# One more V block of the outer rounds kept in SBUF, with shared chain buffers

## Chip, cores and metric

The program runs on 1 core of a Trainium2 chip. The metric is the device time of one execution in microseconds (us), as a median of several. A single-core run counts as slow if it is over 1.5% above the fastest of the same kernel.

## The reference

Four layers, A B A B. Only A matters here: a recurrent attention over 64 segments of 32 rows, where each segment sees 8 memory rows that the segment before produced.

```python
def _A_ref(x, mem0, Wq, Wk, Wv, Wo, seg_len):   # Dm 640, 32 heads of 192, 8 memory rows
    mem = mem0
    for s in range(n_seg):                      # 64 segments, strictly in order
        xs = x[:, s * seg_len:(s + 1) * seg_len, :]
        h = jnp.concatenate([mem, xs], axis=1)  # 40 rows
        q, k, v = (jnp.einsum('btd,dhe->bhte', h, W) for W in (Wq, Wk, Wv))
        ...                                     # masked softmax attention
        o = jnp.einsum('bhte,hed->btd', o, Wo)
        mem = o[:, :M, :]                       # the next segment needs these 8 rows
        outs.append(o[:, M:, :])
```

## The kernel before

The four weight matrices do not fit SBUF together. The 32 heads go in 4 rounds of 8. A segment runs rounds 0 1 2 3, the next one 3 2 1 0, so that the outer rounds 0 and 3 alternate and the round at a segment's turn is used twice in a row. Each matrix of a round has 5 blocks of 128 x 1536 bf16 (393 KB). `SLOTS` says how many of them, in the outer rounds, share one slot between rounds 0 and 3 and are reloaded once per segment; all others are resident. Wo of the outer rounds shares one tile, `wo_end`.

```python
SLOTS = {"Q": 3, "K": 3, "V": 4}
...
def load_slot(m, r, b):
    if holds.get((m, b)) != r:
        holds[m, b] = r
        w = PW if m == "Q" else PW // 2
        for h in range(0, PW, w):
            nc.sync.dma_start(out=slot[m, b][:, h:h + w], in_=wview[m][:, b, PW * r + h:PW * r + h + w])
...
def project(hT, ps, m, n, s, steps):     # round n of the segment: 5 blocks, 4 column tiles each
    ...
    if n == 0 and b >= KC - ns:          # the outer block has been read: fetch the other outer round's
        load_slot(m, order[NR - 1], b)
```

One segment, cut to what the change touches:

```python
to_rows(q_or_k("Q", 0), "Q")             # project, copy to `raw` (two buffers), transpose into QT / KT
to_rows(q_or_k("K", 0), "K")
...                                       # V of round 0
for n in range(L):                        # L = 3
    raw = q_or_k("Q", n + 1)
    if n > 0:
        OT = attend(Ep, n - 1)            # PSUM -> OT, 80 columns of each of 6 chunks
        tails_after(n - 1)
        keep_tail(OT, otb, order[n - 1])  # GpSimd copies the 16 fetched columns; one store per segment
    S, E = weigh(False)                   # scores and exp
    to_rows(raw, "Q")
    next_kq(s, n)
    to_rows(q_or_k("K", n + 1), "K")
    sums(S, E); normalise(S, E)           # ones matmul, Ln, Exp, multiply
    if n > 0:
        wo_round(W, order[n - 1], OT, n == 1, False)
        if n == 1:
            load_wo(order[L])             # wo_end: six pieces, last in the DMA queue
    ...                                   # V of the next round
...
wo_round(W, order[L], OT, False, True)    # reads wo_end piece by piece
keep_busy(idle, 3)                        # three idle matmuls
hT = hN                                   # second hT buffer, its 24 own rows transposed earlier
nc.vector.transpose(out=wt, in_=W ...)    # the 8 memory rows
nc.vector.tensor_copy(out=hT[:, :, 0:8], in_=wt[:, :, 0:8])
```

The softmax here doesn't subtract the row's maximum and nothing guards it: scores larger than these inputs give would overflow.

## Time and profile before

| | before |
|---|---|
| time, median of 3 | 4140.39 us (4123.13 to 4148.61) |
| two recurrent stages, first to last hT cast (62 of 64 segments) | 1424 us each |
| traffic | 986 MB, 238 GB/s over the span |
| slot reloads of V | 1072 DMAs of 192 KB |

The page's row for the wo_end matmuls, with busy time and mean ns, then the idle time just before them and what ended it, is

```profile
L767 PE MATMUL ps_w<-wo_end,OT 128*32 128x160 bf16 x12288 | 316.2, 236 | 168.7 <-DMA wo_end<-wo_rows 123.3
```

The idle column, and not the DMA's share of the chain, is the gap that the prediction counts.

### The profile page before, as it was taken

Reading aid. Unit: us, or ns where it says so; the run is one execution under the profiler, and the core shown is the slowest. Engines: PE = TensorE matmul, PEld = TensorE weight load, DVE = VectorE, ACT = ScalarE, POOL = GpSimd, SP = SyncE. Lnnn points to the kernel's source line nnn. Section 1 sums busy time; section 2 is a strip of 40 time slices with the busy share of each in tenths; the row PEclk is TensorE's granted clock in tenths of the full one; section 3 lists DMA queues with packets and bytes.
Section 4 is the critical chain, followed back from the end, with each engine's and each line's share of the span. In section 5 each row is a group of like instructions: output and inputs, shape, how many; then the busy total and the mean of one; then the engine's idle time right before and its main releaser. Section 6 shows DMA issues by size and latency. Waiting matters only on the chain.

```text
span 4141.3 us, 167399 instructions
## 1 busy us (share of the span) xinstructions
PE 3626.9 (88%) x70296; PEld 2253.0 (54%) x70312; DVE 2139.8 (52%) x5054; ACT 1882.1 (45%) x4461; POOL 1595.1 (39%) x4511
## 2 busy tenths in 40 slices
PE   4889999999999999869879799999999999998598
PEld 3655555555555555535357455555555555555353
DVE  4235555555555555445732455555555555553574
ACT  1235555555555555415312355455545455554252
POOL 1024544454455455330000345445545555542400
PEclk9999999999999999979989999999999999999798
DMA  8878888888888888830077888888878888887200
GB/s 260 250 230 286 273 283 277 280 281 277 283 278 284 275 286 293 285 89 1 31 251 213 268 278 282 265 287 284 286 266 284 275 293 282 282 277 242 86 1 26
DMA packets 642175, 986.34 MB, mean 238 GB/s; under 512 B 152202, under 2 KB 468106, under 8 KB 641418
## 3 DMA queue, kind: packets, MB, share of 16 engines
q1 hardware_dynamic: 497546, 861.82, 61.2%
q0 software_dynamic: 55936, 60.51, 5.3%
q10 hardware_dynamic: 87936, 53.30, 4.7%
q8 instruction: 551, 9.03, 0.9%
q14 instruction: 206, 1.69, 0.1%
HBM read 907.09 MB, written 72.09 MB: 236 GB/s over the span
## 4 chain that ended last, share of the span: by engine, by line
PE 63%; DMA 25%; DVE 4%; issue 3%; ACT 3%; POOL 1%; SPq 1%; ACTq 1%; POOLq 0%; DVEq 0%
PE ps_qk L702 21%; DMA wo_end<-wo_rows 15%; PE ps_v L702 8%; PE ps_w L767 6%; PE ps_pre L613 4%; PE ps_s L742 3%; PE ps_o L750 3%; DMA wslotV<-in_A_Wv_dram 3%; PE ps_qk L342 2%; PE ps_s L794 2%; PE pp L923 2%; PE ps_s L737 2%; PE ps_pre L628 2%; DMA kqb<-wo_mid 2%; PE ps_wo L455 2%
## 5 line engine op out<-in xcount | busy, mean ns | idle before, releaser
L702 PEld LDWEIGHTS <-hT 128*32 128x32 bf16 x30720 | 752.7, 98 | 528.2 <-issue 86.6
L702 PE MATMUL ps_qk<-w_res,hT 128*32 128x384 bf16 x14336 | 783.5, 332 | 1.3 <-issue 0.9
L712 ACT ACTIVATE raw<-ps_qk 128x384 bf16<-128x384 f32 x1024 | 501.7, 490 | 570.4 <-PE ps_qk L702 568.4
L767 PEld LDWEIGHTS <-OT 128*32 128x32 bf16 x24576 | 432.5, 97 | 321.1 <-issue 242.7
L685 POOL DMA_DIRECT2D Vp<-vb x512 | 261.5, 511 | 765.4 <-PE ps_o L750 286.7
L767 PE MATMUL ps_w<-wo_end,OT 128*32 128x160 bf16 x12288 | 316.2, 236 | 168.7 <-DMA wo_end<-wo_rows 123.3
L673 POOL DMA_DIRECT2D kqb<-kqb x512 | 290.6, 568 | 335.4 <-DMA kqb<-wo_mid 162.7
L717 DVE STREAM_TRANSPOSE KT<-raw 128x384 bf16<-128x384 bf16 x512 | 296.1, 578 | 177.2 <-ACT raw L712 173.4
L720 DVE STREAM_TRANSPOSE QT<-raw 128x256 bf16<-128x256 bf16 x512 | 228.0, 445 | 298.7 <-ACT raw L712 287.7
L731 DVE CAST Vp<-ps_v 64x384 bf16<-64x384 f32 x512 | 286.1, 559 | 139.0 <-ACT Vp L729 126.7
L702 PE MATMUL ps_v<-w_res,hT 128*32 128x384 bf16 x6144 | 345.0, 329 | 1.7 <-issue 1.5
L678 POOL COPY QT<-kqb 128x64 bf16<-128x64 bf16 x512 | 123.2, 241 | 564.9 <-PE ps_s L742 562.5
L756 DVE CAST OT<-ps_o 128x240 bf16<-128x240 f32 x512 | 208.8, 408 | 244.2 <-PE ps_o L750 228.0
L801 DVE TENSOR_TENSOR E<-E,ps_s 80x320 bf16<-80x320 bf16 x512 | 247.6, 484 | 145.3 <-ACT ps_s L800 145.1
L729 ACT ACTIVATE Vp<-ps_v 64x384 bf16<-64x384 f32 x512 | 246.1, 481 | 162.4 <-PE ps_v L702 162.3
L750 PEld LDWEIGHTS <-Vp 80*128 80x128 bf16 x4096 | 181.9, 100 | 188.7 <-issue 127.6
L750 PE MATMUL ps_o<-E,Vp 80*128 80x80 bf16 x4096 | 252.7, 203 | 32.2 <-DVE Vp L731 23.4
L767 PE MATMUL ps_w<-wo_mid,OT 128*32 128x160 bf16 x12288 | 266.1, 234 | 4.3 <-issue 3.8
L755 ACT ACTIVATE OT<-ps_o 128x240 bf16<-128x240 f32 x512 | 188.2, 368 | 166.7 <-PE ps_o L750 162.0
L780 ACT ACTIVATE E<-ps_s 80x320 bf16<-80x320 f32 x512 | 221.3, 432 | 87.0 <-PE ps_s L742 72.0
L702 PE MATMUL ps_v<-wslotV,hT 128*32 128x384 bf16 x4096 | 245.4, 334 | 2.5 <-DMA wslotV<-in_A_Wv_dram 2.2
L774 PE MATMUL ps_idle<-wo_mid,ident 128*128 128x384 bf16 x1024 | 242.5, 340 | 1.5 <-issue 1.5
(146 smaller groups left out, 5824.6 us busy)
## 6 DMA issues: line engine op xcount, KB each, us to landing
wo_end<-wo_rows SPq DMA_DIRECT2D x780, 320.0 KB
wslotV<-in_A_Wv_dram SPq DMA_DIRECT2D x1072, 192.0 KB
wslotK<-in_A_Wk_dram SPq DMA_DIRECT2D x804, 192.0 KB
wslotQ<-in_A_Wq_dram SPq DMA_DIRECT2D x402, 384.0 KB
kqb<-wo_mid ACTq DMA_DIRECT2D x16, 1536.0 KB
kqb<-kqb POOLq DMA_DIRECT2D x512, 48.0 KB, 5.0
vb<-wo_end ACTq DMA_DIRECT2D x128, 112.0 KB
Vp<-vb POOLq DMA_DIRECT2D x512, 28.0 KB, 4.8
```

The lines of the kernel that those rows point to most:

```text
L673: nc.gpsimd.dma_start(out=kqb[:], in_=self.kqb_d[s, :, r, :])
L685: nc.gpsimd.dma_start(out=Vs[n % 2][64:80, :], in_=self.vb_d[s, r].rearrange("g t f -> (g t) f"))
L702: nc.tensor.matmul(o[32 * g:32 * g + 32, 0:384], lhsT=hT[:, b, :], rhs=rhs, start=(i == 0), stop=(i == KC - 1), tile_position=(0, 32 * g), ...
L712: nc.scalar.activation(out=raw[:], in_=ps[:, 0:384], func=ACT.Copy)
L717: nc.vector.transpose(out=KT[:, :, 0:64], in_=raw[:, :].rearrange("p (c j) -> p c j", j=64))
L720: nc.vector.transpose(out=QT[:, :, 0:4:3, 0:64], in_=rv[:, :, 0:3:2, :])
L729: nc.scalar.activation(out=o, in_=i, func=ACT.Copy)
L731: nc.vector.tensor_copy(out=o, in_=i)
L750: nc.tensor.matmul(O[x][:, 80 * i:80 * i + 80], lhsT=Vs[n % 2][0:80, 448 * x + k:448 * x + k + 128], rhs=E[0:80, 160 * x + 80 * e:160 * x ...
L767: nc.tensor.matmul(W[32 * g:32 * g + 32, 0:160], lhsT=OT[:, c, q:q + 32], rhs=w[:, 640 * i + 160 * g:640 * i + 160 * g + 160], start=(firs ...
L774: nc.tensor.matmul(ps[:, 0:384], lhsT=self.ident[:, :], rhs=wo_mid[:, 0:384], start=True, stop=True, skip_group_check=True)
L801: nc.vector.tensor_tensor(out=E[0:80, 0:320], in0=E[0:80, 0:320], in1=rc, op=ALU.mult)
```

## The change

The aim is to reload three V blocks per segment, not four. One more resident V block for each of rounds 0 and 3, less the slot they shared, needs 3072 B more per partition. It is found by using one buffer where two were, and by putting rows in unused partitions of the V tiles.

```diff
-SLOTS = {"Q": 3, "K": 3, "V": 4}
+SLOTS = {"Q": 3, "K": 3, "V": 3}
...
-        ones = const.tile([P, 80], BF16, name="ones_blk")
+        ones = const.tile([P, 1], BF16, name="ones_blk")          # read with a stride of 0
...
-            Hx = sp.tile([P, 2, 160], BF16, name="Hx")
+            xr, orow = [t[96:P, 0:640] for t in Vs]                # rows 96 to 127 of the V tiles
...
-                hT = sp.tile([P, KC, 32], BF16, name="hT", tag="hT", bufs=2)
-                nc.vector.transpose(out=hT[:, :, :], in_=Hx[:, s % 2, :].rearrange(...))
+            def hx_transpose(hT, gs):                              # one hT buffer, four transposes
+                for g in gs:
+                    nc.vector.transpose(out=hT[32 * g:32 * g + 32, :, :], in_=xr[:, 160 * g:160 * g + 160]...)
...
+            def keep_rows(W):                                      # four ACT copies of 32 partitions, one store
+                    nc.scalar.activation(out=orow[:, 160 * g:160 * g + 160], in_=W[32 * g:32 * g + 32, 0:160], ...)
...
-                raw = sp.tile([P, 384], BF16, name="raw", tag="raw", bufs=2)
+                raw = sp.tile([P, 384], BF16, name="raw", tag=tag)   # one buffer; K of round 0 takes OT's
...
-                OT = sp.tile([P, 6, 80], BF16, name="OT", tag="OT")
+                OT = sp.tile([P, 6, 64], BF16, name="OT", tag="OT")
...
-            def keep_tail(OT, otb, r):
-                nc.gpsimd.tensor_copy(out=otb[:, r, :, :], in_=OT[:, :, 64:80])
+            def keep_tail(o, late=False):                          # fetched columns straight from PSUM
+                ... nc.scalar.activation / nc.vector.tensor_copy(out=otb[:, 0:3, :], in_=o[0][:, :, 64:80])
+                nc.vector.tensor_copy(out=otb[:, 3:6, :], in_=o[1][:, :, 64:80])
+            def store_tail(otb, s, r):                             # four stores of 24 KB per segment
...
-                normalise(S, E)                                     # last round: VectorE multiplies, then copies its V rows
-                v_rows(pv, L)
+                v_rows(pv, L, "x")                                  # VectorE's V rows first
+                normalise(S, E)
+                v_rows(pv, L, "a")                                  # ScalarE's V rows
...
-    (next segment's hT transposed before the last V projection)
+                hx_transpose(hT, range(1))                          # before the last attend
+                ...
+                hx_transpose(hT, range(1, 4))                       # after it
```

More of the change, by code (lines that the diff above doesn't have):

```diff
@@ L645, in A_chain @@
             Vs = [sp.tile([P, 896], BF16, name=f"Vp{i}") for i in range(2)]
-            Hx = sp.tile([P, 2, 160], BF16, name="Hx")
-            for i, t in enumerate((KT, QT, *Vs, Hx)):
+            xr, orow = [t[96:P, 0:640] for t in Vs]
+            for i, t in enumerate((KT, QT, *Vs)):
                 (nc.vector if i % 2 else nc.gpsimd).memset(t[:], 0.0)
             xv = xn_dram.rearrange("(s t) d -> t s d", t=32)
-            av = at_dram.rearrange("(s t) d -> t s d", t=32)
             def rounds(s):
@@ L658, in load_rows, with new_hT, store_rows @@
             def load_rows(s):
-                for g in range(4):
-                    nc.gpsimd.dma_start(out=Hx[32 * g + 8:32 * g + 32, :, :], in_=xv[0:24, s:s + 2, 160 * g:160 * g + 160])
-            def hx_transpose(s):
-                hT = sp.tile([P, KC, 32], BF16, name="hT", tag="hT", bufs=2)
-                nc.vector.transpose(out=hT[:, :, :], in_=Hx[:, s % 2, :].rearrange("p (j b) -> p b j", b=KC))
-                return hT
-            def store_rows(s, ob):
-                for g in range(4):
-                    nc.gpsimd.dma_start(out=av[0:24, s:s + 2, 160 * g:160 * g + 160], in_=ob[32 * g + 8:32 * g + 32, :, :])
+                nc.gpsimd.dma_start(out=xr[8:32, :], in_=xn_dram[32 * s:32 * s + 24, :])
+            def hx_transpose(hT, gs):
+                for g in gs:
+                    nc.vector.transpose(out=hT[32 * g:32 * g + 32, :, :],
+                                        in_=xr[:, 160 * g:160 * g + 160].rearrange("p (j b) -> p b j", b=KC))
+            def new_hT():
+                return sp.tile([P, KC, 32], BF16, name="hT", tag="hT")
+            def keep_rows(W):
+                for g in range(4):
+                    nc.scalar.activation(out=orow[:, 160 * g:160 * g + 160], in_=W[32 * g:32 * g + 32, 0:160], func=ACT.Copy)
+            def store_rows(s):
+                nc.gpsimd.dma_start(out=at_dram[32 * s:32 * s + 24, :], in_=orow[8:32, :])
             def load_kqb(s, r):
@@ L708, in values, with to_raw @@
                 project(hT, pv, "V", n, s, steps)
-            def to_raw(ps):
-                raw = sp.tile([P, 384], BF16, name="raw", tag="raw", bufs=2)
+            def to_raw(ps, tag):
+                raw = sp.tile([P, 384], BF16, name="raw", tag=tag)
                 nc.scalar.activation(out=raw[:], in_=ps[:, 0:384], func=ACT.Copy)
@@ L722, in to_rows, with v_rows @@
                     nc.vector.transpose(out=QT[64:P, :, 2, 0:64], in_=rv[64:P, :, 1, :])
-            def v_rows(pv, n):
+            def v_rows(pv, n, which="ax"):
                 for x in range(2):
+                    if "ax"[x] not in which:
+                        continue
                     o = self.two_heads(Vs[n % 2][0:64, 448 * x:448 * x + 448])
@@ L752, in attend @@
                                          stop=(k == 192), skip_group_check=True)
-                OT = sp.tile([P, 6, 80], BF16, name="OT", tag="OT")
-                OTf = OT[:, :, :].rearrange("p c q -> p (c q)")
-                nc.scalar.activation(out=OTf[:, 0:240], in_=O[0][:, 0:240], func=ACT.Copy)
-                nc.vector.tensor_copy(out=OTf[:, 240:480], in_=O[1][:, 0:240])
-                return OT
-            def keep_tail(OT, otb, r):
-                nc.gpsimd.tensor_copy(out=otb[:, r, :, :], in_=OT[:, :, 64:80])
+                OT = sp.tile([P, 6, 64], BF16, name="OT", tag="OT")
+                o = [x[:, 0:240].rearrange("p (i q) -> p i q", q=80) for x in O]
+                nc.scalar.activation(out=OT[:, 0:3, :], in_=o[0][:, :, 0:64], func=ACT.Copy)
+                nc.vector.tensor_copy(out=OT[:, 3:6, :], in_=o[1][:, :, 0:64])
+                return OT, o
+            def keep_tail(o, late=False):
+                otb = sp.tile([P, 6, 16], BF16, name="otb", tag="otb", bufs=2)
+                if late:
+                    nc.vector.tensor_copy(out=otb[:, 0:3, :], in_=o[0][:, :, 64:80])
+                else:
+                    nc.scalar.activation(out=otb[:, 0:3, :], in_=o[0][:, :, 64:80], func=ACT.Copy)
+                nc.vector.tensor_copy(out=otb[:, 3:6, :], in_=o[1][:, :, 64:80])
+                return otb
+            def store_tail(otb, s, r):
+                nc.gpsimd.dma_start(out=self.otb_d[s, :, 96 * r:96 * r + 96], in_=otb[:, :, :].rearrange("p c t -> p (c t)"))
             def wo_round(W, r, OT, first, last):
@@ L778, in weigh @@
                 S = scores()
-                E = sp.tile([P, 384], BF16, name="E3", tag="raw", bufs=2) if last else sp.tile([P, 320], BF16, name="E", tag="E")
+                E = sp.tile([P, 384], BF16, name="E3", tag="raw") if last else sp.tile([P, 320], BF16, name="E", tag="E")
                 nc.scalar.activation(out=E[0:80, 0:320], in_=S[0:80, 0:320], func=ACT.Exp, scale=scale)
@@ L793, in sums @@
             def sums(S, E):
-                nc.tensor.matmul(S[0:80, 0:320], lhsT=self.ones_blk[0:80, :], rhs=E[0:80, 0:320], start=True, stop=True,
+                nc.tensor.matmul(S[0:80, 0:320], lhsT=ap3(self.ones_blk[0:80, :], [list(self.ones_blk[0:80, :].ap[0]), [0, 80]]), rhs=E[0:80, 0:320], start=True, stop=True,
                                  skip_group_check=True)
@@ L801, in normalise @@
                 nc.vector.tensor_tensor(out=E[0:80, 0:320], in0=E[0:80, 0:320], in1=rc, op=ALU.mult)
-            for g in range(4):
-                nc.gpsimd.dma_start(out=Hx[32 * g:32 * g + 8, 0, :], in_=self.A_mem0[:, 160 * g:160 * g + 160])
+            nc.gpsimd.dma_start(out=xr[0:8, :], in_=self.A_mem0[:, :])
             load_rows(0)
@@ L812, in A_chain @@
             kqs.append(load_kqb(0, rounds(0)[2]))
-            hT = hx_transpose(0)
-            otb = ob = None
+            hT = new_hT()
+            hx_transpose(hT, range(4))
+            load_rows(1)
             for s in range(NSEG):
-                if s % 2 == 0:
-                    ob_old, ob = ob, sp.tile([P, 2, 160], BF16, name="ob", tag="ob")
                 W = pop.tile([P, 512], F32, name="ps_w", tag="w")
@@ L824, in q_or_k @@
                     project(hT, ps, m, n, s, range(KC))
-                    return to_raw(ps)
+                    return to_raw(ps, "OT" if m == "K" and n == 0 else "raw")
                 def v_banks():
@@ L838, in A_chain @@
                 if s > 0:
-                    nc.gpsimd.dma_start(out=self.otb_d[s - 1], in_=otb[:, :, :, :].rearrange("p r c t -> p (r c t)"))
-                    if s % 2 == 0:
-                        store_rows(s - 2, ob_old)
+                    store_rows(s - 1)
                 pv = v_banks()
@@ L844, in A_chain @@
                 v_rows(pv, 0)
-                otb = sp.tile([P, NR, 6, 16], BF16, name="otb", tag="otb")
                 Ep = None
@@ L849, in A_chain @@
                     if n > 0:
-                        OT = attend(Ep, n - 1)
+                        OT, o = attend(Ep, n - 1)
                         tails_after(n - 1)
-                        keep_tail(OT, otb, order[n - 1])
                     S, E = weigh(False)
                     to_rows(raw, "Q")
+                    if n > 0:
+                        otb = keep_tail(o)
                     next_kq(s, n)
+                    if n > 0:
+                        store_tail(otb, s, order[n - 1])
                     to_rows(q_or_k("K", n + 1), "K")
@@ L870, in A_chain @@
                 S, E = weigh(True)
-                if s + 1 < NSEG:
-                    hN = hx_transpose(s + 1)
                 pv = v_banks()
                 project(hT, pv, "V", L, s, range(3))
-                OT = attend(Ep, L - 1)
+                OT, o = attend(Ep, L - 1)
                 tails_after(L - 1)
-                keep_tail(OT, otb, order[L - 1])
+                otb = keep_tail(o, True)
                 next_kq(s, L)
+                store_tail(otb, s, order[L - 1])
                 sums(S, E)
                 project(hT, pv, "V", L, s, range(3, KC))
+                v_rows(pv, L, "x")
                 normalise(S, E)
-                v_rows(pv, L)
+                v_rows(pv, L, "a")
+                if s + 1 < NSEG:
+                    hT = new_hT()
+                    hx_transpose(hT, range(1))
                 wo_round(W, order[L - 1], OT, False, False)
@@ L885, in A_chain @@
                 keep_busy(idle, 2)
-                OT = attend(E, L)
+                OT, o = attend(E, L)
                 tails_after(L)
-                keep_tail(OT, otb, order[L])
-                if s % 2 == 0 and s + 2 < NSEG:
-                    load_rows(s + 2)
+                if s + 1 < NSEG:
+                    hx_transpose(hT, range(1, 4))
+                    if s + 2 < NSEG:
+                        load_rows(s + 2)
                 keep_busy(idle, 3)
@@ L894, in A_chain @@
                 if s + 1 < NSEG:
-                    hT = hN
-                    wt = sp.tile([P, KC, 32], F32, name="wt", tag="raw", bufs=2)
+                    wt = sp.tile([P, KC, 32], F32, name="wt", tag="raw")
                     nc.vector.transpose(out=wt[:, :, :], in_=W[:, 0:160].rearrange("p (j b) -> p b j", b=KC))
                     nc.vector.tensor_copy(out=hT[:, :, 0:8], in_=wt[:, :, 0:8])
-                nc.scalar.activation(out=ob[:, s % 2, :], in_=W[:, 0:160], func=ACT.Copy)
-            nc.gpsimd.dma_start(out=self.otb_d[NSEG - 1], in_=otb[:, :, :, :].rearrange("p r c t -> p (r c t)"))
-            store_rows(NSEG - 2, ob)
+                store_tail(keep_tail(o), s, order[L])
+                keep_rows(W)
+            store_rows(NSEG - 1)
     def A_post(self, at_dram, li, wo_mid, wo_end, big):
```

## The prediction

> **What bounds the kernel now.** I read the page's slices and chain first, then the stages, then one segment instruction by instruction, then the waits of that segment's end.
>
> Parts 2 and 4 of the page:
>
> ```profile
> PE   4889999999999999869879799999999999998598
> DMA  8878888888888888830077888888878888887200
> GB/s 260 250 230 286 273 283 277 280 281 277 283 278 284 275 286 293 285 89 1 31 251 213 268 278 282 265 287 284 286 266 284 275 293 282 282 277 242 86 1 26
> ...
> PE 63%; DMA 25%; DVE 4%; issue 3%; ACT 3%; POOL 1%; SPq 1%; ACTq 1%; POOLq 0%; DVEq 0%
> ```
>
> TensorE and the DMA engines are both nearly full through most of the span, and the chain alternates between them. The two recurrent stages (64 segments each) fill 285 to 1709 us and 2337 to 3761 us; their table of busy times is
>
> ```profile
> 285.00:1709.00 1424.00, 1319.56 (x31249) 818.86 (x31247) 785.42 (x1922) 738.41 (x1798) 712.87 (x2042) 0.98 0.84 281
> 2337.00:3761.00 1424.00, 1317.51 (x31249) 817.74 (x31247) 785.68 (x1922) 738.25 (x1798) 712.83 (x2042) 0.98 0.84 281
> ```
>
> The columns are span, then busy time of PE, PEld, DVE, ACT and POOL, then granted clock, DMA share and GB/s. So 2848 of 4141 us lie here, DMA 84% busy, PE 93%. The chain of waits in one segment names the loop (start us, us, what):
>
> ```profile
> 1017.66 0.57 PE ps_v L702 x9
> 1018.23 6.65 DMA wo_end<-wo_rows
> 1024.89 0.04 issue
> 1024.93 0.35 PE ps_w L767 x8
> 1025.30 0.36 DVE wt L897
> 1025.68 0.20 DVE hT L898
> ```
>
> The next segment cannot begin before its memory rows (hT), which come from the whole ps_w sum, which needs the last piece of wo_end, which stands last in the DMA queue behind this segment's Q, K and V blocks. The 6.65 us is no stall: TensorE worked through most of it. Its true stall is the idle before the wo_end matmuls, in the timeline of PE:
>
> ```profile
> 1021.64 0.78 PE L767 MATMUL ps_w<-wo_end,OT 128*32 128x160 bf16 x24
> 1023.09 0.32 PE L767 MATMUL ps_w<-wo_end,OT 128*32 128x160 bf16 x8 [0.66 <-DMA wo_end<-wo_rows]
> 1024.20 0.32 PE L767 MATMUL ps_w<-wo_end,OT 128*32 128x160 bf16 x8 [0.80 <-DMA wo_end<-wo_rows]
> 1024.93 0.32 PE L767 MATMUL ps_w<-wo_end,OT 128*32 128x160 bf16 x8 [0.40 <-DMA wo_end<-wo_rows]
> ```
>
> Here it is 1.86 us. Summed by group over the first stage, then over the second:
>
> ```profile
> L767 PE MATMUL ps_w<-wo_end,OT 128*32 128x160 bf16 x5952 | 152.6, 237 | 78.5 <-DMA wo_end<-wo_rows 54.0 <-issue 22.0 <-ACT OT L755 1.4
> ...
> L767 PE MATMUL ps_w<-wo_end,OT 128*32 128x160 bf16 x5952 | 152.1, 235 | 78.0 <-DMA wo_end<-wo_rows 58.2 <-issue 19.2
> ```
>
> That is 156 us. **It is the most that fewer bytes can give directly.** DMA sets the period, but TensorE is only some 1.3 us per segment behind it.
>
> From the trace's records I cut both stages at the hT cast into 124 segments: mean period 22.97 us; first weight packet 1.69 us after the cast; stream from there to the last wo_end packet 19.67 us (6.31 MB, 321 GB/s, engines 95% busy, standard deviation 0.79 us); 1.61 us from there to the next cast. The DMA engines rest only in the turn between segments.
>
> **What the Trainium skill says.** "DMA: Bandwidth & Descriptors", section Issuing engines are not separate DMA queues: transfers from SP, ACT and GpSimd share 16 engines and interleave. The trace agrees: the segments' stream is 95% busy over all queues together, so a byte less anywhere in it shortens it. The same page, Specifications, sets 512 B as the smallest line-rate transfer. The trace does not show a penalty at 320 B: the 15 KB row transfers have packets of four such rows at a median 55 ns (23 B/ns), the old 768 B tail rows run at 4608 B in 206 ns (22 B/ns). The new 192 B rows are untested here. "TensorE: Matmul & The Clock Gate", What's actually happening: an activity window of 3413 ns halves the clock after idling. The clock records agree in form: they hold 0.5 stretches of 3.4 us, and the stages' mean is 0.98. "PSUM — Partial Sum Buffer", PSUM bank collisions: two engines' reads of one bank are kept apart by waits. It shows: ACT's ob copy waited for DVE's wt, both reading ps_w, for 426 us in the wait list.
>
> **The change part by part.**
> 1. *One V block (round 0 and round 3) stays resident; V reloads 3 blocks a segment, not 4.* Removed: two DMAs of 192 KB, that is 256 packets of 1536 B. At 71 ns a packet (mean in the records) over 16 engines: 1.14 us busy, 1.20 us of stream at 95%. By rate: 0.393 MB at 321 GB/s is 1.22 us. All of it precedes wo_end in the queue. Over two layers of 64 segments that is 50 MB of 986.
> 2. *Tail rows leave by four DMAs of 24 KB instead of one of 96 KB.* Same bytes, but the old one went at the segment's turn (POOL issued it at 1024.74 us), where the engines were resting; three of the new ones fall into the stream: 74 KB, 0.23 us. The row loads and stores become 24 rows of 1280 B in place of 320 B pieces, and some of the loads that ran beside the last wo_end pieces (packets up to 0.3 us long there) get simpler: I credit 0.1 us. **Stream shorter by 1.1 us net.**
> 3. *raw has one buffer instead of two (K of the first round borrows OT's).* ACT's copy of K must now wait for DVE's three Q transposes. In the segment shown, ACT began it at 1015.96 and DVE ended at 1016.06: with the hand-over 0.15 us later in each of three rounds. Scores follow KT's end (1017.07) with PE at 1017.21, and the attend at 1009.52 follows E's end at 1009.40, so about 0.1 us of TensorE delay in two places: 0.15 us.
> 4. *hT has one buffer, filled by four 32-partition transposes instead of one of 128.* One takes 352 ns now and its free size does not change, so 1.4 us, placed after the last V projection. Three follow the OT copy (ends near 1021.7), so DVE is free near 1022.7; without a DMA stall ps_w would end near 1022.6. 0.1 us.
> 5. *Tail copies go from POOL (275 ns each, gone) to ACT and DVE, from PSUM; OT is copied 192 wide, not 240.* Both have idle there (ACT 52%, DVE 55% busy in the stages); the OT copies, on the path, get some 0.04 us shorter.
> 6. *The row copy becomes four ACT copies of 32 partitions*, about 1.2 us in place of 0.3, after DVE's wt. ACT's next work came 1.29 us after the hT cast began (1002.43 to 1003.72): it just fits. No cost.
> 7. The ones matrix as a stride-0 column: one weight load of 114 ns a round, loaded ahead; no cost.
>
> TensorE's own loop thus grows by about 0.2 us (3, 4, less 5). The matmul count does not change.
>
> **Sum.** For each of the 124 segments, gain = stall less the larger of 0.2 and (stall less 1.1). The 156 us of stalls are uneven (quartiles 0.76, 1.29, 1.76 us), so the mean gain is 0.78 us rather than 0.9: 98 us over 126 turns. Clock: 51 segments with a halved stretch average 23.38 us, the other 73 22.69 us; 51 x 0.69 is 35 us, and with the stalls mostly gone I expect under half of it back, 15 us. The preparation stage reloads one block less per layer: 2 us. Together 115 us: **4025 us**, 2.8% less.
>
> **Rivals.**
> - *TensorE's chain becomes the bound early.* If the single raw buffer, the hT transposes and the row copies cost 0.5 us a segment, the same sum gives 75 us, and without clock gain 4063 us, within 2%. For it: slacks of 0.1 us in four places. Against it: each is a small shift beside idle time.
> - *The 192 B rows are slow.* If each took twice its bytes' time the stream shortens by 0.8 us; with 0.2 us on TensorE 76 us remain; with 2 us of preparation and half the clock gain (7 us) that is about 4055 us. Against it: 320 B rows show no loss.
> - *Proportional DMA gain.* If DMA alone set the period, 1.2 us x 128 and the 15 us of clock would give 3970 us. Against it: the stall is below 1.1 us in over a third of the segments, so TensorE catches up.
> - *Hidden anyway:* the chain's 25% DMA overstates; but 156 us of real idle exist, so "same" needs the new costs above.
>
> **Range and chances.** Low end: 1.22 us net, no TensorE cost, all clock loss back: 118 + 35 + 2 us, 3985 us, and some luck: 3975. High end: 0.95 us, 0.5 us cost, no clock gain: 70 us, 4070 us, and run-to-run spread (4123 to 4149 before): 4080. The 2% line is 4058 us, which leaves 33 us of margin against a doubt of some 40: faster 0.77, same 0.22, slower 0.01.
>
> **What would show it.** Right: wslotV moves a quarter less; the stream falls to about 18.6 us; idle before the wo_end matmuls falls from 156 to 50 to 75 us; period near 22.1 us; more segments wait for nothing; clock at or above 0.98. Wrong step 2: the new tail stores' packets exceed 100 ns each. Wrong steps 3 to 6: PE idle before ps_s, ps_o or the first ps_qk, or wt waiting for DVE's own transposes. The prediction fails above all if a new wait on raw, OT or hT puts over 0.5 us in every segment.

## The result

| | before | after |
|---|---|---|
| median | 4133.17 us, 4 runs | 4009.80 us, 4 runs (3987.02 to 4029.03) |
| ratio, 95% interval | 1 | 0.9696 (0.9633 to 0.9760) |
| stages, first to last hT cast | 1424.2, 1424.2 us | 1360.7, 1356.7 us |
| V reloads of 192 KB | 1072 | 804 |
| traffic | 986 MB | 935 MB |

Ratios are the mean time of one kernel's fast runs over the mean of the other's in the same rounds, so they are not quite the ratio of the medians. The changed kernel is faster by 3.0%, 123 us by the medians; its result is correct. Of the 127 us between the two profiled spans (4141.3 and 4014.4 us), 131 us came from the stages, and 4 us were lost outside them.

Slices and chain of the page after:

```profile
PE   4889999999999999869879799999999999998598
DMA  7777888788887888730076788788887887885200
GB/s 266 242 240 255 272 272 280 270 281 284 271 281 265 287 284 270 253 91 1 35 256 206 256 273 279 264 288 281 276 282 267 282 283 262 280 275 194 87 1 27
...
PE 62%; DMA 18%; DVE 6%; ACT 6%; issue 4%; POOL 2%; SPq 1%; ACTq 1%; POOLq 0%; DVEq 0%
```

The rate hardly changes (277 and 276 GB/s in the stages, 281 before); there is less to move. In the chain DMA falls from 25 to 18%, and DVE and ACT together rise from 7 to 12%: in some segments the chain now runs through the softmax and the copies. The row of the wo_end matmuls on the page after, and the stages' table:

```profile
L782 PE MATMUL ps_w<-wo_end,OT 128*32 128x160 bf16 x12288 | 291.2, 236 | 64.6 <-DMA wo_end<-wo_rows 32.4
...
285.00:1640.00 1355.00, 1292.20 (x31124) 813.19 (x31120) 887.89 (x2409) 811.77 (x2162) 674.82 (x1851) 0.99 0.82 277
2264.00:3619.00 1355.00, 1290.32 (x31136) 812.85 (x31136) 888.02 (x2410) 811.45 (x2162) 675.78 (x1853) 0.99 0.82 276
```

The idle time before them fell from 168.7 to 64.6 us over the whole span. Their busy time fell too, from 316.2 to 291.2 us, with the same count and the same mean of 236 ns: the matmuls overlap more when fewer waits break their row. So the idle column leaves out a part of what a wait costs. DVE has about 100 us more to do in each stage, ACT 73 us, POOL 38 us less; TensorE has the same matmuls. The waits of the segment's end, in the timeline of PE after:

```profile
1029.81 0.45 PE L756 MATMUL ps_o<-E,Vp 80*128 80x80 bf16 x8 [0.33 <-DMA Vp<-vb]
1030.09 0.66 PE L789 MATMUL ps_idle<-wo_mid,ident 128*128 128x384 bf16 x3
1030.67 0.97 PE L782 MATMUL ps_w<-wo_end,OT 128*32 128x160 bf16 x40
1032.50 0.32 PE L782 MATMUL ps_w<-wo_end,OT 128*32 128x160 bf16 x8 [0.85 <-DMA wo_end<-wo_rows]
```

Here five of the six pieces of wo_end are there in time and only the last is awaited, 0.85 us; in the segment of the prediction three of six were late.

To see where a segment's time goes, the trace's records were cut at the hT cast, as in the prediction: 124 segments, means in us. "First" runs from the cast to the first weight packet, "stream" from there to the last wo_end packet, "turn" from there to the next cast; the three add up to the period. "Stall" is TensorE's idle time before the wo_end matmuls, and the last column counts the segments that hold over 0.1 us of a halved-clock stretch, in which the records grant TensorE half its clock. The experiments are in the same table.

| kernel | period | first | stream | turn | stall | halved |
|---|---|---|---|---|---|---|
| before | 22.97 | 1.69 | 19.67 | 1.61 | 1.26 | 51 |
| after | 21.91 | 1.63 | 18.51 | 1.77 | 0.45 | 18 |
| e1, all but the V block | 22.86 | 1.66 | 19.61 | 1.59 | 1.08 | 40 |
| e2, the V block's bytes alone | 21.76 | 1.63 | 18.39 | 1.74 | 0.47 | 9 |
| e3, before, one block more | 24.32 | 1.79 | 21.05 | 1.48 | 1.76 | 95 |
| e4, after, one block less | 21.44 | 1.60 | 17.34 | 2.50 | 0.06 | 2 |
| e9, after again | 21.80 | 1.59 | 18.39 | 1.82 | 0.44 | 5 |
| e11, after with two repairs | 21.74 | 1.62 | 18.39 | 1.74 | 0.45 | 11 |
| e12, before with fillers | 23.14 | 1.63 | 19.80 | 1.71 | 0.74 | 24 |

The stream lost 1.16 us, the turn gained 0.16 us, and that is nearly the whole change of the period, 1.06 us. In the segments with all 504 matmul records (88 before, 105 after), TensorE reaches the last round's wo_end matmuls only 0.05 us sooner than before, and from their start to their end it takes 0.96 us less.

### The profile page after: what moved, and what is told of

Same layout as the page of the kernel before. It is cut to its first block, busy times and chain, and to the rows that moved or that the text cites. A ratio compares the mean times of both kernels' runs of the same rounds, so it can differ in the third digit from the quotient of the medians.

```text
span 4014.4 us, 168003 instructions
## 1 busy us (share of the span) xinstructions
PE 3588.7 (89%) x70296; PEld 2252.9 (56%) x70312; DVE 2357.3 (59%) x6078; ACT 2040.1 (51%) x5229; POOL 1516.4 (38%) x4119
## 4 chain that ended last, share of the span: by engine, by line
PE 62%; DMA 18%; DVE 6%; ACT 6%; issue 4%; POOL 2%; SPq 1%; ACTq 1%; POOLq 0%; DVEq 0%
PE ps_qk L706 18%; DMA wo_end<-wo_rows 10%; PE ps_w L782 8%; PE ps_v L706 6%; PE ps_pre L613 4%; PE ps_o L756 4%; PE ps_s L748 3%; PE ps_s L809 2%; PE ps_qk L342 2%; PE pp L939 2%; PE ps_s L743 2%; PE ps_pre L628 2%; DMA kqb<-wo_mid 2%; PE ps_wo L455 2%; PE ps_idle L789 2%
## 5 line engine op out<-in xcount | busy, mean ns | idle before, releaser
L706 PEld LDWEIGHTS <-hT 128*32 128x32 bf16 x30720 | 741.9, 97 | 493.2 <-DVE hT L914 53.4
L706 PE MATMUL ps_qk<-w_res,hT 128*32 128x384 bf16 x14336 | 769.1, 328 | 1.1 <-ACT otb L770 0.6
L706 PE MATMUL ps_v<-w_res,hT 128*32 128x384 bf16 x7168 | 385.0, 328 | 0.0
L775 POOL DMA_DIRECT2D otb<-otb x512 | 283.8, 554 | 181.7 <-DVE otb L771 137.5
L782 PE MATMUL ps_w<-wo_end,OT 128*32 128x160 bf16 x12288 | 291.2, 236 | 64.6 <-DMA wo_end<-wo_rows 32.4
L762 DVE CAST OT<-ps_o 128x192 bf16<-128x192 f32 x512 | 183.2, 358 | 236.8 <-PE ps_o L756 218.6
L756 PE MATMUL ps_o<-E,Vp 80*128 80x80 bf16 x4096 | 235.3, 202 | 38.7 <-DMA Vp<-vb 9.0
L748 PE MATMUL ps_s<-QT,KT 128*80 128x80 bf16 (+1 forms) x3072 | 234.3, 213 | 19.2 <-DVE KT L721 12.1
```

The costliest lines, as they stand in the source:

```text
L706: nc.tensor.matmul(o[32 * g:32 * g + 32, 0:384], lhsT=hT[:, b, :], rhs=rhs, start=(i == 0), stop=(i == KC - 1), tile_position=(0, 32 * g), ...
L748: nc.tensor.matmul(S[0:80, c0:c0 + 80 * (q1 - q0)], lhsT=KT[:, 3 * x + i, :], rhs=QT[:, x, q0:q1, :], start=False, stop=(x == 1 and i == 2 ...
L756: nc.tensor.matmul(O[x][:, 80 * i:80 * i + 80], lhsT=Vs[n % 2][0:80, 448 * x + k:448 * x + k + 128], rhs=E[0:80, 160 * x + 80 * e:160 * x ...
L775: nc.gpsimd.dma_start(out=self.otb_d[s, :, 96 * r:96 * r + 96], in_=otb[:, :, :].rearrange("p c t -> p (c t)"))
L782: nc.tensor.matmul(W[32 * g:32 * g + 32, 0:160], lhsT=OT[:, c, q:q + 32], rhs=w[:, 640 * i + 160 * g:640 * i + 160 * g + 160], start=(firs ...
```

## The experiments

**Which part brings the gain, and which part costs? (e1, e2)** The theory: all gain comes from the bytes, and the moved buffers and copies cost TensorE about 0.2 us, hidden. The rival: lighter GpSimd work and larger row transfers bring some of it.

e1 is the changed kernel with the old number of slots.

```diff
-SLOTS = {"Q": 3, "K": 3, "V": 3}
+SLOTS = {"Q": 3, "K": 3, "V": 4}
```

> Everything of the change except the resident V block: four V blocks are still reloaded per segment. Theory (the gain is the bytes; the moved buffers and copies cost TensorE some 0.2 us a segment, hidden under the DMA stall): 0 to -0.5% against the kernel before, so 4110 to 4135 us. Rival (the moved copies, the larger rows and the lighter POOL give part of the gain themselves): 4060 to 4090 us. Rival (the moved parts cost more than they hide): over 4160 us.

Measured: 4126.43 us against 4139.00, ratio 0.9970 (0.9944 to 0.9997), correct. All the rest of the change together is worth about 0.3%, by the interval 0.03 to 0.56%; the stream is 19.61 us, against 19.67.

e2 is the kernel before, with one V block never reloaded in the stages. Its result is wrong (relative error 0.022).

```diff
-                        load_slot(m, order[NR - 1], b)
+                        load_slot(m, order[NR - 1], b, m == "V" and b == KC - 1)   # true: mark as loaded, no DMA
```

> The kernel before with one V block of the slots never reloaded in the recurrent stages (its result is wrong on purpose: round 3 reads round 0's block). Bytes alone, with the old buffers. Theory: the stream shortens by 1.2 us, and without the extra 0.2 us on TensorE the time is 10 to 30 us under the changed kernel: 3980 to 4000 us. Rival (part of the gain comes from the rest of the change): 4030 to 4060 us.

Measured: 4007.25 us, ratio 0.9683 (0.9641 to 0.9726). The bytes alone bring the gain of the whole change (0.9696) within the intervals. The advantage of 10 to 30 us that I expected over the changed kernel is not resolved: the intervals overlap.

**Is a block worth the same in both directions? (e3, e4)** If DMA alone sets the period, yes; if TensorE is close behind, the next block brings less and one more block costs more.

```diff
-SLOTS = {"Q": 3, "K": 3, "V": 4}
+SLOTS = {"Q": 3, "K": 3, "V": 5}      # e3: before, five V blocks reloaded
```

> The kernel before with one more V block reloaded per segment (five instead of four), a correct result. Theory (DMA sets the period in nearly all segments before): the step in this direction is the full 1.2 us x 128 = 154 us, or more with clock loss: 4285 to 4310 us. Rival (TensorE and DMA share the bound evenly, so a block is worth the same 123 us in both directions): 4250 to 4260 us.

Measured: 4333.42 us, ratio 1.0460 (1.0423 to 1.0498), correct: 194 us by the medians, more than the 146 to 171 us expected. In the trace 167 us of the 197 us lie in the stages (1505.8 and 1509.5 us against 1424.2 twice); the stream grew by 1.38 us, not 1.2. Outside the stages the span grew by 30 us, which my figure left out.

e4 is the changed kernel with the skip of e2, so that only two V blocks are reloaded (wrong result, relative error 0.022).

> The changed kernel with one more V block never reloaded in the recurrent stages (wrong result on purpose). Theory (TensorE is close behind: 57 us of wo_end stall are left): at most 57 us less, I expect 35 to 50 us: 3960 to 3975 us. Rival (DMA alone sets the period): another 123 us, 3890 us. Rival (TensorE is already the bound): under 20 us less.

Measured: 3955.38 us, ratio 0.9562 (0.9532 to 0.9592): 54 us under the changed kernel's median of 4009.80 (each measured against the kernel before), more than the 35 to 50 us expected and just under the 57 us of stall. Its row of the wo_end matmuls shows that the stall is used up:

```profile
L784 PE MATMUL ps_w<-wo_end,OT 128*32 128x160 bf16 x12288 | 268.3, 234 | 13.3 <-DMA wo_end<-wo_rows 6.3 <-issue 6.2
```

The stream fell by another 1.17 us, but the turn grew from 1.77 to 2.50 us: the data now lie there before TensorE asks. A block was worth 194, 123 and 54 us in turn. From the kernel before to e4 the stages lost 190 us (124 times 22.97 less 21.44), more than their 156 us of stall.

**What does TensorE's own loop cost? (e5, e6, e7)** With no slot and no wo_end reload in the stages (wrong results, relative error 0.033 to 0.034), DMA is 11% busy there and only TensorE's loop is left, called the floor below.

```diff
-                        load_slot(m, order[NR - 1], b)
+                        load_slot(m, order[NR - 1], b, True)     # e5 on before, e6 on after
-                            load_wo(order[L])
```

> The kernel before with no slot and no wo_end reload at all in the recurrent stages (wrong result on purpose): TensorE's own loop, without DMA. From the segments without stall (21.0 to 21.3 us a segment): 126 x (22.97 - 21.15) = 230 us less, 3900 to 3930 us. It is the reference for the next two runs.

Measured: 3816.55 us, ratio 0.9237. I had expected 3900 to 3930 us, a clear miss. The period is 20.71 us, not the 21.15 us that I had read from segments without a stall, and 40 us went outside the stages (their first and last segments among them). A segment without a stall is no measure of the loop without DMA: the wo_end matmuls are not the only ones that wait while the weights stream. In the changed kernel's 47 segments with under 0.1 us of stall, attend's matmuls have 0.51 us of idle time before them; with DMA off (e6) they have 0.13 us.

> The same for the changed kernel. Prediction (steps 3 and 4: moved buffers cost TensorE 0.2 us a segment): 25 us over the floor of before. Rival (they cost nothing, the narrower OT copies and the lighter POOL pay for them): within 10 us. Rival (0.5 us): 63 us over it.

Measured: 3844.96 us, ratio 0.9307: 28 us over e5, 20.87 us a segment. The predicted 0.2 us (25 us) is right in its sum.

```diff
-        raw = sp.tile([P, 384], BF16, name="raw", tag=tag)
+        raw = sp.tile([P, 384], BF16, name="raw", tag=tag, bufs=2 if tag == "raw" else 1)   # e7, on e6
-        return to_raw(ps, "OT" if m == "K" and n == 0 else "raw")
+        return to_raw(ps, "raw")
```

The buffers of E3 and wt follow raw's, and four V slots make the room.

> The changed kernel's floor with two raw buffers as before and K's first copy back in raw (four V slots to make room; nothing is reloaded, wrong result on purpose). If the single raw buffer costs 0.15 us a segment (step 3), this is 15 to 20 us under the changed kernel's floor; if the cost lies in hT and the tail (step 4), within 6 us of it.

Measured: 3800.78 us, ratio 0.9198: 44 us under e6 and 16 us under e5, 20.50 us a segment. So the single raw buffer costs 0.37 us (20.87 less 20.50), over twice what step 3 allowed, and all the rest of the change shortens TensorE's loop by 0.21 us (20.71 less 20.50) instead of costing 0.06 us (0.1 less 0.04). The chain of waits of e6, in the second round, shows where (start us, us, what):

```profile
1009.38 0.27 PE ps_s L811
1009.66 0.49 ACT raw L718
1010.14 0.33 ACT ps_s L816
1010.47 0.02 issue
1010.49 0.42 ACT ps_s L817
1010.91 0.02 issue
1010.93 0.49 DVE E L818
1011.43 0.04 issue
1011.47 0.45 PE ps_o L758 x8
```

and the same round of e7:

```profile
1015.36 0.26 PE ps_s L811
1015.62 0.93 PE ps_v L708 x20
1016.54 0.81 PE ps_qk L708 x20
1017.35 0.39 PE ps_o L758 x8
```

With two buffers the chain passes from the ones matmul (L811) through TensorE's own projections to attend (L758): 1.99 us from start to start. With one, ACT's K copy starts late, Ln and Exp queue behind it, DVE's multiply ends late, and attend waits for that: 2.09 us. (The chain puts the copy's start down to L811, which it does not read; what it had to wait for, VectorE's last Q transpose, ended at 1009.54 us in the timeline, 0.11 us before it.) Matching the 504 matmuls of a segment one by one takes the 0.37 us apart: in the means over 124 segments, 0.15 us are lost at this attend and 0.21 us before the last round's scores, which wait for KT, whose transpose follows a late K copy in the same way. Elsewhere, up to the segment's last matmul, under 0.01 us is lost. A second place is the segment's end; the chain of e6 there is

```profile
1002.71 0.36 DVE hT L664
1003.07 0.01 issue
1003.09 0.36 DVE hT L664
1003.45 0.01 issue
1003.46 0.35 DVE hT L664
1003.82 0.03 issue
1003.85 0.36 DVE wt L914
```

wt waits for DVE's own three transposes, as step 4 had it. The first projection of the next segment waits 0.16 us a segment in e6, against 0.08 us in e5.

What shortens TensorE's loop shows in the rows of the attend matmuls, first e5, then e7:

```profile
L752 PE MATMUL ps_o<-E,Vp 80*128 80x80 bf16 x4096 | 257.8, 204 | 32.8 <-DVE Vp L733 32.3
L758 PE MATMUL ps_o<-E,Vp 80*128 80x80 bf16 x4096 | 235.9, 203 | 4.6
```

The wait for VectorE's copy of the V rows (Vp) is gone, and by the end of the last attend e7 is 0.26 us ahead of e5. In the last round the change makes this copy before the softmax multiply and not after it. That the order does it is read from the traces; no run tries it singly.

**Can the lost part be had back? (e8 to e11)** The OT buffer is free for the K copy of the second round as well; it needs no new memory.

```diff
-        return to_raw(ps, "OT" if m == "K" and n == 0 else "raw")
+        return to_raw(ps, "OT" if m == "K" and n < 2 else "raw")
```

> The changed kernel with the K copy of the second round put in the OT buffer too, which is free then, so that it need not wait for the Q transposes (correct result). The wait of the first attend on the softmax chain should go. If TensorE's loop matters in the segments without stall: 5 to 15 us less, 3995 to 4005 us. If DMA hides it: no change within 5 us.

Measured: 3998.39 us, ratio 0.9672 (0.9647 to 0.9697), correct. As the changed kernel was not in that call, both were run again in one call, with a third that also takes a second hT transpose ahead of the last attend:

```diff
-                hx_transpose(hT, range(1))
+                hx_transpose(hT, range(2))         # e11, on e10
-                hx_transpose(hT, range(1, 4))
+                hx_transpose(hT, range(2, 4))
```

> The changed kernel once more, to share its rounds with the next two: 4000 to 4020 us, 2.7 to 3.4% under the kernel before.

> K's second copy in the OT buffer again, now in the same rounds as the changed kernel. The first run had 3998 us. Theory (the single raw buffer costs TensorE 0.35 us a segment on its floor, a third or more of it in this round): 5 to 15 us under the changed kernel. Rival (the first difference was the spread between calls): within 4 us.

> As the run before, and two of the four hT transposes go ahead of the last attend instead of one, into 0.7 us where VectorE idles. In the segments without stall the memory rows' transpose waits for VectorE by about 0.1 us: if that counts, 3 to 8 us under the run before; if not, within 3 us.

| | median | ratio to before |
|---|---|---|
| e9, changed kernel | 4014.03 us | 0.9688 (0.9661 to 0.9716) |
| e10, K copy in OT | 3999.19 us | 0.9661 (0.9635 to 0.9687) |
| e11, and the transpose moved | 3996.54 us | 0.9646 (0.9620 to 0.9672) |

By the five runs of each, e10 is 11 us under e9, with a 95% interval from the spread of the runs of about 12 us each way, so not quite resolved; but in the traces attend's start in the second round, matched in the same way, is 0.165 us earlier than in the changed kernel, as e7 had it. e11 is 17.5 us under e9, give or take 12 us, which is clear; e11 against e10 (6 us) is not resolved. e11 has the lowest median of the correct versions, 3.5% under before.

**Does the halved clock cost time? (e12)** Before, 51 segments held a halved-clock stretch and were 0.69 us longer than the others. If idling causes it and it costs time, idle matmuls inside the stall should give some back.

```diff
+                    if filler is not None and i in (6, 8, 10):   # ahead of the last three wo_end pieces
+                        keep_busy(filler, 1)
```

> The kernel before with three more idle matmuls, one ahead of each of the last three wo_end pieces, inside the stall (correct result). They cost TensorE up to 0.5 us where the stall is shorter than that (about 6 us in all). If the halved clock of 51 segments costs 35 us and idling causes it, they give back 15 to 30 us: 4105 to 4120 us against 4131 to 4139. If the halved clock is hidden under the DMA wait as well, no gain: within 10 us of the kernel before, or above it.

Measured: 4158.01 us against 4140.11, ratio 1.0032 (0.9997 to 1.0067), correct. The halved segments fell from 51 to 24, the clock of the first stage rose:

```profile
285.00:1709.00 1424.00, 1348.21 (x31219) 825.36 (x31211) 780.53 (x1911) 733.71 (x1786) 708.32 (x2027) 0.99 0.83 279
```

It was 0.98 in that stretch before. TensorE did get faster: from the hT cast to the first scores 3.68 us on average, 3.99 before. But the time did not fall, and the stream stayed (19.80 us). Whether a restored clock is worth anything while DMA sets the period, the run does not settle, because the fillers cost time as well. Before, the halved segments have the same stream as the others (19.69 and 19.66 us) but a longer start (1.80 against 1.61 us) and turn (1.88 against 1.42 us), together 0.65 us; in e12 the turn of the segments without a halved stretch grew from 1.42 to 1.61 us. Estimated from these, 27 fewer halved segments would save 18 us, if the clock is what lengthens them, and the fillers would take 19 us in the other 100.

## Why the prediction was right

It said 4025 us and 2.8% less; 4009.8 us and 3.0% less were measured, inside the range. By its steps:

1. **The V block's bytes.** Predicted 1.20 us of stream. e2 shows 1.28 us (19.67 to 18.39), and the whole gain with it. Right.
2. **Tail stores and row transfers, 0.1 us net loss.** With e1 the stream is 19.61 us against 19.67: no loss seen. The 192 B rows are not slow: in the stages after, packets of eight such rows take a median 65 ns, as long as the 1536 B weight packets took before. The net stream, 1.16 us shorter, was predicted as 1.1 us.
3. **One raw buffer, 0.15 us.** Wrong in size: 0.37 us on the floor. The two kinds of place were right, scores behind KT and attend behind E, but each alone loses at least what the step allowed for both: 0.21 us at the last round's scores and 0.15 us at the second round's attend, where a late K copy is carried on through Ln, Exp and the multiply, which are in line on ACT and DVE.
4. **One hT buffer, 0.1 us.** The mechanism is shown (wt behind DVE's transposes), with 0.08 us more waiting.
5. **Copies moved, 0.04 us gain.** Not seen: up to the last attend, e7's matmuls start within 0.02 us of e5's. The gain that outweighs the costs has a source that no step names. It is VectorE's copy of the last round's V rows, now made earlier: 0.26 us by the end of the last attend (e7 against e5). The sum of 3 to 5, 0.2 us predicted, is 0.16 us a segment: an unforeseen gain cancelled the error of step 3, which is luck.
6. **Row copies and ones column, no cost.** No wait of TensorE on them appears in the wait list after. (The 426 us that the prediction quotes for ACT's ob copy behind wt is ACT's whole idle time there; wt itself took 0.36 us a segment.)
7. **From stall to time.** Stall 156 to 56 us in the stages: 100 us, predicted 98. The period fell by less than the stream, 1.06 against 1.16 us. But the stall is not "the most that fewer bytes can give", and TensorE is not "only some 1.3 us per segment behind" (its floor, 20.71 us, is 2.26 us under the period): the stages lost 131 us, and 190 us in e4, in part because a wait also costs overlap (busy time of the wo_end matmuls, 25 us less in the whole span). The rivals "DMA alone" and "hidden anyway" are refuted by e4 and e2, slow 192 B rows by the packets of step 2, and a chain 0.5 us longer by e6 (0.16 us).
8. **The clock, 15 us.** Not shown. After, 18 and 5 halved segments in two profiles instead of 51, so more of them went than the prediction gave back (under half of 35 us). From the hT cast to the first scores the changed kernel takes 3.69 us, 3.99 before; how much of that reaches the period was not measured apart, and e12 does not settle it. TensorE's own loop is no part of the gain: it grew by 0.16 us. How the 31 us beyond the stall divide between overlap and clock stays open.

Open: with the weights streaming TensorE needs more than on the floor, 21.44 us in e4 against 20.87 us in e6. Some of it is idle time that the profile puts down to nothing ("issue"): from 300 to 1500 us, e4's wait list has 12.8 us of it before the ps_w matmuls and 4.5 us before attend, and e6's list has none.

## What to carry to other kernels

When a transfer and an engine take turns in setting a loop's period, count the engine's idle time before the awaited tile per iteration, and credit the smaller of that and the transfer's saving as a first estimate; here it gave 98 us where the stages lost 131, in part because the idle time leaves out lost overlap. The next saving of the same size is worth less. Memory freed by dropping a second buffer has a price in the work that queues behind it on other engines, which the bound of the moment may hide; measure it with the transfers switched off. Then look whether another buffer is free at that moment, which here, with one transpose moved as well, gave 17.5 us back without new memory.

## What the Trainium skill lacked or had wrong

- "DMA: Bandwidth & Descriptors", Specifications, sets 512 B as the least transfer for line rate. Here rows of 192 B from SBUF to DRAM took no longer than long ones: eight in a packet of 1536 B, median 65 ns, as 1536 B rows of weights from DRAM (65 ns); e1 lost nothing. Such rows are a small part of the traffic.
- "TensorE: Matmul & The Clock Gate", HAM oscillation, gives as a rule to avoid idle gaps over some 3.4 us; the section after it tells of a kernel whose short pauses made the clock oscillate, without their length. In the first stage of the kernel before no single wait of TensorE was longer than 2.74 us, and yet 51 of 124 segments (both stages) held a halved stretch; in the changed kernel, with smaller stalls, 18 and 5.
- The same page does not say whether halving costs time while DMA sets the period. The runs leave it open: in e12 the halved segments fell from 51 to 24 while the time went from 4140 to 4158 us, but the fillers' own cost is in that.
- No page gives a way to tell, within one loop, the iterations that DMA bounds from those that TensorE bounds; here the worth of one and the same 393 KB went from 194 to 123 to 54 us.
